# Seven conditional expert blocks, one after the other or one inside the other

## The chip, the cores and the metric

The kernel runs on one core of a Trainium2 chip. Its time is the device time of one execution, in microseconds (us); three executions of the kernel before took 800.02, 800.99 and 801.18 us, so the median is 800.99. A core has five engines that run their own instruction lists and wait for each other through semaphores: TensorE (PE, matmuls), VectorE (DVE), ScalarE (ACT), GpSimd (POOL, which also issues the gathers and scatters) and SyncE (SP, which issues the plain DMAs).

## What is computed

Three stages follow each other: a linear attention over four sequences of 576 positions, a gated dense layer, and a layer of eight experts of which each token uses one. The experts matter here. A token goes to the expert with the largest logit; each expert takes at most `capacity` tokens, 576 with these inputs:

```python
logits = x @ w_gate
expert_idx = np.argmax(logits, axis=1)
probs = softmax(logits);  gate_w = probs[np.arange(N), expert_idx]
# the first `capacity` tokens of each expert, in order, are kept
h = np.maximum(np.einsum('ecd,edf->ecf', disp, w1), 0.0)      # 512 -> 1024
y = np.einsum('ecf,efd->ecd', h, w2)                          # 1024 -> 512
out[i] = gate_w[i] * y[expert_idx[i], pos[i]]                 # 0 for tokens that are not kept
```

There are 2304 tokens. With these inputs four of the eight experts get 576 tokens each and the other four get none; no token is dropped. The kernel finds this out while it runs.

## The kernel before

Attention and the dense layer are written out as one long list of instructions without branches. While their last matmuls run, the tokens are routed: a table in DRAM gets for each expert the row numbers of its tokens, and a small tile `plan` gets the list of active experts, their counts and the number of active ones, `nact`.

The expert with the most tokens is worked on first, without a condition. The other experts are seven blocks in a Python loop, j = 1 to 7, each in a `tc.If(nact > j)` of its own (line 996). The number of the expert is read from `plan` by SP when its weights are loaded. With these inputs `nact` is 4: blocks 1, 2 and 3 are entered, 4 to 7 are not.

A block (`body`, L961) works on 256 + 320 rows of one expert in two calls of `part` (L188), the second in a condition on the count (L984). Each part runs over eight slices f of the 1024 hidden columns: a group of matmuls into `ph`, ScalarE's relu (L235) and VectorE's remainder (L238) into `h`, and the second group of matmuls from `h` into `yo`. Each float32 matmul is done as three matmuls of a high and a low half (`mm3`, L115 to L117). In between, `ew_dma` and `ew_split` load the next expert's weights and split them (`es`, `eu`, L123 to L135), `gather` fetches rows (`gr`, L167), and `turn` transposes them. A part ends with `emit` (L211): ScalarE scales `yo` into `y` (L214), and POOL scatters the rows of `y` into the output (L144). The last 64 rows are held as two halves; SP copies one half to the other's partitions (`z`, L217), VectorE adds them (L219).

The order of all instructions is the order in which the program is written (`manual_schedule`). Tiles come out of pools: 13 large `unit` buffers, 4 for `h`, 2 for weights on arrival, 2 for the tables, 5 + 3 PSUM banks, 7 for rows.

How a condition is built matters. Each engine has its own branch (COMPARE_AND_BRANCH). A block that is entered raises semaphores as its instructions end, and what follows the block waits for fixed counts. So an engine that skips a block runs a short list in its place, which raises the same semaphores by the same amounts: EVENT_SEMAPHORE instructions, and on POOL one INC_SWDGE_SEM for the semaphores of its own DMAs. It stands under the line of the condition, L996, and ends in an unconditional branch to what follows the block.

Of the kernel before, what the change touches and what calls it, by code (L numbers as in the profile page):

```python
# [8 lines left out]
F32 = mybir.dt.float32  # L9
F32R = mybir.dt.float32r  # L10
BF16 = mybir.dt.bfloat16
I32 = mybir.dt.int32
# [6 lines left out]
P = 128  # L19
B, H, S, D = 4, 8, 576, 64  # L20
NT = B * S
DM = H * D
DFF = 1536
NE = 8
FE = 1024
NC = DM // P
NFC = DFF // P
BLK = 384
# [4 lines left out]
RA = 256  # L33
RB = 320
# [33 lines left out]
go4.0 hl5.1* ac4.2 ac3.2* ac4.0*  # L68
"""
F64_MIN = struct.unpack("<f", struct.pack("<I", 897 << 20))[0]  # L70


def program(tc, ins, outs):
    nc = tc.nc
    ctx = ExitStack()
    with ctx:
# [4 lines left out]
        def unit(shape, dt, name):  # L81
            return units.tile(shape, dt, name=name, tag="unit")
# [20 lines left out]
        hp = ctx.enter_context(tc.tile_pool(name="hp", bufs=4))  # L103
        stg = ctx.enter_context(tc.tile_pool(name="stg", bufs=2))
        tbp = ctx.enter_context(tc.tile_pool(name="tbp", bufs=2))
        psa = ctx.enter_context(tc.tile_pool(name="psa", bufs=5, space=PSUM))
        pso = ctx.enter_context(tc.tile_pool(name="pso", bufs=3, space=PSUM))
# [58 lines left out]
        def gather(st, i, idx, g, n, rows=NT):  # L166
            nc.gpsimd.indirect_dma_start(  # L167
                out=g[:n],
                out_offset=None,
                in_=x2d[0:rows],  # L170
                in_offset=bass.IndirectOffsetOnAxis(ap=idx, axis=0),
                bounds_check=rows - 1,
                oob_is_err=False,
            )
            st[i] = g

        def turn(st, i, x, k, n=P):
            g = st.pop(i)
            pt = ps(f"tg{i}").rearrange("p (c t) -> p c t", c=NC)
            for c in range(NC):  # L180
                nc.tensor.transpose(pt[:, c, :n], g[:n, c * P : (c + 1) * P], ident[:n, :n])
            o = k * P
            nc.scalar.copy(x[:, :, 0, o : o + n], pt[:, :, :n])
            nc.vector.tensor_tensor(
                x[:, :, 1, o : o + n], pt[:, :, :n], x[:, :, 0, o : o + n].bitcast(F32), op=ALU.subtract
            )
# [74 lines left out]
        with ExitStack() as s2:  # L261
# [178 lines left out]
            def cb(f, i):  # L440
                tf, mag = ld["c", f, i]
                nc.vector.scalar_tensor_tensor(tf, mag, F64_MIN, tf, op0=ALU.is_ge, op1=ALU.mult)

# [254 lines left out]
            for token in FIRST.split():  # L698
                name = token.rstrip("*")
# [82 lines left out]
            for b in range(5):  # L782
                k = (4, 5, 7, 9, 11)[b]
# [12 lines left out]
            for i, (b, fs, mode) in enumerate(steps):  # L796
# [7 lines left out]
                k = i % NBLK  # L804
# [28 lines left out]
            xb = unit([P, NC, 2, 3 * P], F32R, "xb0")  # L833
# [60 lines left out]
        xgp = s3.enter_context(tc.tile_pool(name="xgp", bufs=2, reuse_waits="tile"))  # L894
        grp = s3.enter_context(tc.tile_pool(name="grp", bufs=7, reuse_waits="tile"))

        def g_tile(i):
            return grp.tile([P, DM], F32, name=f"gr{i}", tag="gr")

        def next_tables(e):  # L900
            st = {}
            fetch(st, "ta", e, 0, 2)
            fetch(st, "tb", e, RA, 2, rest=True)
            for i in range(2):
                gather(st, i, st["ta"][:, i, 0:1], g_tile(i), P)
            return st

        def turn_a(st):
            st["xa"] = xgp.tile([P, NC, 2, RA], F32R, name="xa", tag="xa")
            for i in range(2):  # L910
                turn(st, i, st["xa"], i)
# [4 lines left out]
        def work(ew, e, fs, lag):  # L916
            at = {}
            for i, f in enumerate(fs):
                at.setdefault(0 if i < 2 else lag[i - 2], []).append(lambda f=f: ew_dma(ew, e, f))
                at.setdefault(lag[i], []).insert(0, lambda f=f: ew_split(ew, f, both))  # L920
            return at

        def hooks(at, extra=None):
            def hook(f):
                if f == 0:
                    for w in at.get(0, ()):
                        w()
                if extra is not None:
                    extra(f)

            def after(f):
                if f > 0:
                    for w in at.get(f, ()):
                        w()

            return hook, after

        ew, st = {}, {}
# [19 lines left out]

        nact = st.pop("nact")

        def body(j, st, ew):  # L961
            more = j + 1 < NE
            cj = nc.values_load(plan[0:1, NE + j : NE + j + 1], min_val=0, max_val=NT)
            xb = unit([P, NC, 2, RB], F32R, "xb")
            nst, new = {}, {}

            def extra(f):
                if f == 0:
                    for i in range(3):
                        n = P if i < 2 else HALF  # L970
                        gather(st, 2 + i, st["tb"][:n, i, 0:1], g_tile(2 + i), n)
                if f == 1 and more:
                    nst.update(next_tables(nexp[j]))
                if 4 <= f <= 6:
                    turn(st, f - 2, xb, f - 4, P if f < 6 else HALF)
                if f == 7 and more:
                    turn_a(nst)

            half = work(new, nexp[j], range(4), (2, 4, 5, 6)) if more else {}
            part(st["xa"], RA, (P, P), ew, st["ta"], grp, "gr", *hooks(half, extra))  # L980
            if more:
                for k in (3, 4, 5):
                    new["u", k] = unit([P, 3, 2, 512], F32R, f"eu{k}")
            with tc.If(cj > RA) as big:  # L984
                half = work(new, nexp[j], range(4, 8), (1, 3, 5, 6)) if more else {}
                part(xb, RB, (P, P, HALF), ew, st["tb"], grp, "gr", *hooks(half))
            if more:
                with big.Else():
                    half = work(new, nexp[j], range(4, 8), (1, 2, 3, 4))
                    for f in range(5):  # L990
                        for w in half.get(f, ()):
                            w()
            return nst, new

        for j in range(1, NE):
            with tc.If(nact > j):  # L996
                st, ew = body(j, st, ew)


def layout(inputs):  # L1000
# [37 lines left out]
```

## Time and profile before

| | |
|---|---|
| median of three executions | 800.99 us |
| the profiled execution, its own time | 800.0 us |
| its span, first to last instruction | 798.2 us |
| TensorE busy | 759.5 us, 95% of the span |
| VectorE, ScalarE, GpSimd busy | 402.2, 278.8, 273.2 us |
| mean granted TensorE clock over the span | 0.987 |

The span is what the trace shows of one execution; 1.8 us of the execution's time lie around it. Branches and semaphore instructions are not counted as busy, so an engine may be idle in the table and still be at work in its instruction list. The view of one source line shows those instructions too, with a q behind the engine's name (POOLq, and PEldq for TensorE's list).

### The profile page before, as it was taken

What the parts mean: (1) busy time and instruction counts of PE and PEld (TensorE: products, weight loads), DVE (VectorE), ACT (ScalarE), POOL (GpSimd) and SP (SyncE); (2) the same over time, 40 slices, a digit from 0 to 9 for tenths busy, and PEclk for the clock granted to TensorE, in tenths of its full rate; (3) what the DMA queues carried; (4) which work ended last, traced back from release to release, by engine and by line L of the source; (5) the groups of instructions that cost most, each with busy time, mean ns of one, the idle gap of its engine ahead of it and who ended that gap; (6) DMA issues with size and microseconds to landing.
All of it is one profiled execution on the core that took longest, in us unless ns stands there. A gap on an engine that the chain in (4) does not pass through costs nothing. (4 is left out here: it accounts for less than half of the span.)

```text
span 798.2 us, 11945 instructions
## 1 busy us (share of the span) xinstructions
PE 759.5 (95%) x4400; PEld 698.0 (87%) x4400; DVE 402.2 (50%) x826; ACT 278.8 (35%) x537; POOL 273.2 (34%) x276
## 2 busy tenths in 40 slices
PE   6989999999999999999999999999999999999980
PEld 5988998999999999999989999999888888888870
DVE  7999966345454454544863323347724422433330
ACT  6756833322222222222332112223325533524430
POOL 5473713123232232322331313222535524425220
PEclk9999999999999999999999999999999999999995
DMA  9952020111010110101211011143255524515311
GB/s 305 364 172 83 28 79 28 31 53 53 27 54 27 53 50 31 53 28 53 80 67 40 2 41 41 53 134 117 62 150 176 191 80 127 159 53 182 129 41 37
DMA packets 34798, 70.53 MB, mean 88 GB/s; under 512 B 6528, under 2 KB 8704, under 8 KB 34720
## 3 DMA queue, kind: packets, MB, share of 16 engines
q1 hardware_dynamic: 31008, 59.40, 22.7%
q0 software_dynamic: 3712, 10.13, 4.0%
q8 instruction: 43, 0.70, 0.4%
q14 instruction: 35, 0.29, 0.1%
HBM read 59.45 MB, written 9.55 MB: 86 GB/s over the span
## 5 line engine op out<-in xcount | busy, mean ns | idle before, releaser
L491 POOL TENSOR_TENSOR h<-sg,h 128x384 fp32r<-128x384 f32 x70 | 77.6, 1110 | 242.5 <-ACT h L487 236.3
L483 DVE TENSOR_TENSOR sg<-sg,pv 128x384 f32<-128x384 f32 x72 | 39.7, 553 | 125.3 <-PE pv L117 100.6
L115 PE MATMUL pg<-xT,w 128*128 128x384 f32 x288 | 99.0, 344 | 0.0
L115 PE MATMUL pv<-xT,w 128*128 128x384 f32 x288 | 98.1, 341 | 0.1
L117 PE MATMUL pv<-xT,w 128*128 128x384 f32 x288 | 96.6, 336 | 1.5 <-POOL w L451 1.5
L116 PE MATMUL pg<-xT,w 128*128 128x384 f32 x288 | 96.7, 336 | 0.0
L117 PE MATMUL pg<-xT,w 128*128 128x384 f32 x288 | 96.5, 335 | 0.0
L116 PE MATMUL pv<-xT,w 128*128 128x384 f32 x288 | 96.4, 335 | 0.0
L117 PE MATMUL po<-w,h 128*128 128x512 f32 x216 | 86.0, 398 | 0.0
L115 PE MATMUL po<-w,h 128*128 128x512 f32 x216 | 85.2, 394 | 0.0
L116 PE MATMUL po<-w,h 128*128 128x512 f32 x216 | 85.1, 394 | 0.0
L479 ACT ACTIVATE sg<-pg 128x384 f32<-128x384 f32 x72 | 35.3, 490 | 129.4 <-PE pg L117 129.3
L451 POOL TENSOR_TENSOR w<-cv,w 128x512 fp32r<-128x512 f32 x34 | 45.1, 1325 | 98.7 <-ACT w L447 97.6
L487 ACT CAST h<-sg 128x384 fp32r<-128x384 f32 x68 | 34.9, 514 | 111.5 <-DVE sg L483 107.5
L238 DVE SCALAR_TENSOR_TENSOR h<-ph,h 128x64 fp32r<-128x64 f32 (+2 forms) x96 | 31.1, 354 | 84.0 <-ACT h L235 83.6
L135 POOL TENSOR_TENSOR eu<-es,eu 128x512 fp32r<-128x512 f32 x34 | 44.0, 1302 | 85.8 <-ACT eu L134 77.6
L521 DVE TENSOR_TENSOR acc<-acc,po 128x512 f32<-128x512 f32 x78 | 53.1, 687 | 36.5 <-PE po L117 35.3
L235 ACT ACTIVATE h<-ph 128x256 fp32r<-128x256 f32 (+3 forms) x64 | 26.3, 411 | 98.9 <-PE ph L117 61.0
L135 DVE TENSOR_TENSOR eu<-es,eu 128x512 fp32r<-128x512 f32 x46 | 43.1, 948 | 32.7 <-ACT eu L134 32.3
L117 PEld LDWEIGHTS pv<-xT,w 128*128 128x128 f32 x288 | 54.1, 188 | 2.2 <-POOL w L451 2.2
L116 PEld LDWEIGHTS pg<-xT,w 128*128 128x128 f32 x288 | 54.2, 188 | 1.3
L115 PEld LDWEIGHTS pg<-xT,w 128*128 128x128 f32 x288 | 54.1, 188 | 1.4
(201 smaller groups left out, 1667.9 us busy)
## 6 DMA issues: line engine op xcount, KB each, us to landing
es<-in_w SPq DMA_DIRECT2D x80, 256.0 KB, 3.4
s<-in_w SPq DMA_DIRECT2D x30, 512.0 KB, 3.4
q<-in_q SPq DMA_DIRECT2D x18, 256.0 KB, 7.0
x2d<-acc SPq DMA_DIRECT2D x6, 768.0 KB, 3.6
kt<-in_kT SPq DMA_DIRECT2D x3, 1152.0 KB, 8.1
vt<-in_v SPq DMA_DIRECT2D x3, 1024.0 KB, 15.0
raw<-in_w SPq DMA_DIRECT2D x6, 512.0 KB, 11.3
kt<-in_kT SPq DMA_DIRECT2D x4, 288.0 KB, 4.9
```

The costliest lines, as they stand in the source:

```text
L115: nc.tensor.matmul(out, l_hi, r_hi, start=start, stop=False)
L116: nc.tensor.matmul(out, l_hi, r_lo, start=False, stop=False)
L117: nc.tensor.matmul(out, l_lo, r_hi, start=False, stop=stop)
L135: engines[(i + f) % 2].tensor_tensor(u[:, 1], s[:, i], u[:, 0].bitcast(F32), op=ALU.subtract)
L235: nc.scalar.activation(h[:, 0, :used], ph[:, :used], AF.Relu)
L238: nc.vector.scalar_tensor_tensor(dst, ph[:, cols], 0.0, h[:, 0, cols].bitcast(F32), op0=ALU.max, op1=ALU.subtract)
L451: two[eng].tensor_tensor(w[:, i, 1, :], ld.pop(("c", f, i))[0], w[:, i, 0, :].bitcast(F32), op=ALU.subtract)
L479: nc.scalar.activation(pr, gt.pop(("g", b, f)), AF.Sigmoid)
L483: nc.vector.tensor_tensor(pr, pr, gt.pop(("v", b, f)), op=ALU.mult)
L487: alt[eng](h[:, 0], gt["r", b, f])
L491: two[eng].tensor_tensor(h[:, 1], gt.pop(("r", b, f)), h[:, 0].bitcast(F32), op=ALU.subtract)
L521: nc.vector.tensor_tensor(row(b, tt), row(b, tt), otile[b, tt], op=ALU.add)
```

## The change

The seven conditions are nested: block j + 1 stands inside block j, at its end. `chain` calls itself. Where an engine skips block 4, it branches past 5, 6 and 7 too, since they stand inside it: the list that takes the place of block 4 ends in a branch to the end of the kernel.

All tiles that the blocks use are now taken once, ahead of block 1. `Ring` hands out a fixed list of tiles in turn and has the method `tile` of a pool, so that the functions that call it stay as they are; `Tables` does this for the two tables. The number of buffers of each kind is the same as before: 6 + 6 `unit` tiles for two sets of weights and one for `xb`, 4, 2, 5, 3, 7 and 2 + 2 for the others.

```diff
+class Ring:
+    def __init__(self, tiles):
+        self.tiles, self.n = list(tiles), 0
+
+    def tile(self, shape, dt, name, tag):
+        self.n += 1
+        return self.tiles[(self.n - 1) % len(self.tiles)]
...
+        def ring(pool, n, shape, dt, tag, *first):
+            more = [pool.tile(shape, dt, name=f"{tag}r{i}", tag=tag) for i in range(n)]
+            return Ring([*more, *first])
+        sets = [
+            {k: u for k, u in ew.items() if k[0] == "u"},
+            {("u", k): unit([P, 3, 2, 512], F32R, f"ev{k}") for k in range(6)},
+        ]
+        xb1 = unit([P, NC, 2, RB], F32R, "xb1")
+        hp = ring(hp, 4, [P, 2, BLK], F32R, "h")
+        psa = ring(psa, 5, [P, 512], F32, "a")
...
         def body(j, st, ew):
...
-            xb = unit([P, NC, 2, RB], F32R, "xb")
-            nst, new = {}, {}
+            xb = xb1
+            nst, new = {}, dict(sets[j % 2])
...
-            if more:
-                for k in (3, 4, 5):
-                    new["u", k] = unit([P, 3, 2, 512], F32R, f"eu{k}")
...
-        for j in range(1, NE):
+        def chain(j, st, ew):
             with tc.If(nact > j):
-                st, ew = body(j, st, ew)
+                nst, new = body(j, st, ew)
+                if j + 1 < NE:
+                    chain(j + 1, nst, new)
+
+        chain(1, st, ew)
```

Lines move by 19 ahead of `body` and by 34 at the conditions: L984 becomes L1018, L996 becomes L1030, L1034 becomes L1072.

On POOL, at the end of block 6, the kernel before has this row. The four TENSOR_TENSOR are what the condition on the count does if it isn't met; the first ISA is its INC_SWDGE_SEM, and the second, at L996, that of the skipped block 6.

```order
L984 UNCONDITIONAL_BRANCH
L135 TENSOR_TENSOR eu_8928<-es_9181,eu_8928 128x512
L135 TENSOR_TENSOR eu_8928<-es_9184,eu_8928 128x512
L135 TENSOR_TENSOR eu_8929<-es_9191,eu_8929 128x512
L135 TENSOR_TENSOR eu_8929<-es_9198,eu_8929 128x512
L984 ISA
L984 UNCONDITIONAL_BRANCH
L996 ISA
L996 UNCONDITIONAL_BRANCH
L996 COMPARE_AND_BRANCH
L963 TENSOR_LOAD plan
L167 DMA gr_9225<-x2d,tb 128x512
```

The same place on POOL in the changed kernel:

```order
L1018 UNCONDITIONAL_BRANCH
L154 TENSOR_TENSOR eu_5629<-stgr_5752,eu_5629 128x512
L154 TENSOR_TENSOR eu_5629<-stgr_5753,eu_5629 128x512
L154 TENSOR_TENSOR eu_5704<-stgr_5752,eu_5704 128x512
L154 TENSOR_TENSOR eu_5704<-stgr_5753,eu_5704 128x512
L1018 ISA
L1018 UNCONDITIONAL_BRANCH
L1030 COMPARE_AND_BRANCH
L1000 TENSOR_LOAD plan
L186 DMA grr_5765<-x2d,tb 128x512
```

The work keeps its order; the list for the skipped block (L996 ISA and its branch) no longer stands between two blocks.

The end of POOL's list before, from the last block's scatters on; L1034 is the end of the kernel:

```order
L144 DMA out<-y_9651,tb 2304x512
L144 DMA out<-y_9659,tb 2304x512
L144 DMA out<-y_9641,tb 2304x512
L984 UNCONDITIONAL_BRANCH
L984 ISA
L984 UNCONDITIONAL_BRANCH
L996 ISA
L996 UNCONDITIONAL_BRANCH
L1034 ISA
```

And in the changed kernel, where seven pairs of ISA and branch stand behind each other, of which two are shown; the first takes the place of block 7, the last that of block 1 with all that it holds:

```order
L163 DMA out<-grr_5765,tb 2304x512
L163 DMA out<-grr_5766,tb 2304x512
L163 DMA out<-grr_5763,tb 2304x512
L1018 UNCONDITIONAL_BRANCH
L1018 ISA
L1018 UNCONDITIONAL_BRANCH
L1030 ISA
L1030 UNCONDITIONAL_BRANCH
L1030 ISA
L1030 UNCONDITIONAL_BRANCH
```

Every one of the seven branches goes to the end of the kernel, so an engine runs one of the seven lists. The lists for the skipped blocks have moved from between the blocks to the end, and the one for block 4 now raises the semaphores of blocks 4 to 7 together (by 64 to 80 each on POOL, where the one for block 4 before raised them by 16 to 32).

## Rows read from the trace of the kernel before

**Rows 1.** The page's first part: busy us (share of span) xinstructions
```profile
PE 759.5 (95%) x4400; PEld 698.0 (87%) x4400; DVE 402.2 (50%) x826; ACT 278.8 (35%) x537; POOL 273.2 (34%) x276
```

**Rows 2.** Stretches, each engine's busy us: blocks 1, 2, 3, the end
```profile
core 0: us, PE busy (x) PEld busy (x) DVE busy (x) ACT busy (x) POOL busy (x), PEclk, DMA share, GB/s
613.00:667.50 54.50, 54.50 (x329) 48.52 (x328) 20.09 (x38) 22.75 (x46) 21.82 (x19) 1.00 0.38 126
667.50:722.00 54.50, 54.25 (x326) 47.95 (x325) 19.61 (x38) 21.11 (x43) 20.25 (x18) 1.00 0.39 124
722.00:776.20 54.20, 54.01 (x322) 47.40 (x321) 19.56 (x38) 20.81 (x43) 20.70 (x18) 1.00 0.38 124
776.20:798.20 22.00, 0.00 (x0) 0.00 (x0) 0.68 (x1) 0.64 (x1) 3.37 (x3) 0.55 0.18 43
```

**Rows 3.** Timeline, PE: start us, us, engine, line, operation; the last matmul
```profile
775.72 0.39 PE L117 MATMUL yo<-eu,h 128*128 128x512 f32 x1
```

**Rows 4.** Timeline, POOL after 776 us: block 3's last scatters
```profile
776.41 1.00 POOL L144 DMA_INDIRECT out<-y,tb  x1 [5.27 <-ACT y L214]
...
779.48 0.92 POOL L144 DMA_INDIRECT out<-y,tb  x1 [0.30 <-issue]
```

**Rows 5.** L996 on POOL by stretch: duration ns min/median/max, first and last start
```profile
L996 POOLq COMPARE_BRANCH  x1: 45/45/45, 778.8 to 778.8; - x1
...
L996 POOLq EVENT_SEMAPHORE  x4: 17/43/43, 783.8 to 784.3; - x4
L996 POOLq INC_SWDGE_SEM  x1: 1371/1371/1371, 784.4 to 784.4; - x1
L996 POOLq COMPARE_BRANCH  x1: 45/45/45, 785.8 to 785.8; - x1
...
L996 POOLq INC_SWDGE_SEM  x1: 1353/1353/1353, 786.7 to 786.7; - x1
...
L996 POOLq INC_SWDGE_SEM  x1: 1353/1353/1353, 788.8 to 788.8; - x1
...
L996 POOLq INC_SWDGE_SEM  x1: 1353/1353/1353, 791.0 to 791.0; - x1
```

**Rows 6.** L1034, the end of the kernel, on POOL
```profile
L1034 POOLq EVENT_SEMAPHORE  x4: 17/17/17, 797.4 to 798.1; - x4
L1034 POOLq DRAIN  x3: 46/107/4960, 792.4 to 797.9; - x3
```

**Rows 7.** L996 and L1034 in TensorE's list, after 770 us
```profile
L996 PEldq COMPARE_BRANCH  x4: 3825/4421/5667, 773.8 to 788.8; - x4
...
L1034 PEldq DRAIN  x2: 8/8/8, 793.6 to 797.7; - x2
```

**Rows 8.** SP's waits after 776 us: us in total, times, longest
```profile
SPq L996 <- SPq L996: 8.4, 3, 4.0
SPq L1034 <- DMA out<-y,tb: 5.9, 1, 5.9
```

**Rows 9.** L942 on POOL, the skipped block for dropped tokens, and what follows it
```profile
L942 POOLq COMPARE_BRANCH  x1: 45/45/45, 599.2 to 599.2; - x1
L942 POOLq INC_SWDGE_SEM  x1: 728/728/728, 600.1 to 600.1; - x1
...
600.95 1.30 POOL L135 TENSOR_TENSOR eu<-es,eu 128x512 fp32r<-128x512 f32 x1 [1.33 <-DMA out<-y,ta]
```

**Rows 10.** L1026, the start of the kernel, on POOL
```profile
L1026 POOLq DRAIN  x1: 187/187/187, 0.3 to 0.3; - x1
```

**Rows 11.** Waits, 612 to 777 us: PE's, PEld's, VectorE's; SP's to the end
```profile
PE yo L117 <- DVE h L238: 0.3, 1, 0.3
...
PEld tg L181 <- issue: 1.1, 3, 0.4
PEld yo L117 <- DVE h L238: 0.7, 1, 0.7
...
DVE y L219 <- DMA z<-y: 8.7, 2, 5.0
...
SPq L217 <- ACT y L214: 38.0, 3, 12.9
```

**Rows 12.** Timeline, PE: the first matmuls of block 3, and its first `yo`
```profile
721.60 1.59 PE L229 MATMUL ph<-xa,eu 128*128 128x256 f32 x12
...
724.46 0.39 PE L115 MATMUL yo<-eu,h 128*128 128x512 f32 x1
```

More of the change, by code (lines that the diff above doesn't have):

```diff
@@ L70, with __init__, tile @@
 F64_MIN = struct.unpack("<f", struct.pack("<I", 897 << 20))[0]
+class Ring:
[4 more added lines that the diff above has]
+        return self.tiles[(self.n - 1) % len(self.tiles)]
+class Tables:
+    def __init__(self, ta, tb):
+        self.of = {"ta": ta, "tb": tb}
+    def tile(self, shape, dt, name, tag):
+        return self.of[tag].tile(shape, dt, name, tag)
 def program(tc, ins, outs):
@@ L959, in program @@
         nact = st.pop("nact")
+        def ring(pool, n, shape, dt, tag, *first):
[7 more added lines that the diff above has]
+        hp = ring(hp, 4, [P, 2, BLK], F32R, "h")
+        stg = ring(stg, 2, [P, 2, 512], F32, "stg")
+        psa = ring(psa, 5, [P, 512], F32, "a")
+        pso = ring(pso, 3, [P, 512], F32, "o")
+        grp = ring(grp, 7, [P, DM], F32, "gr")
+        xgp = ring(xgp, 1, [P, NC, 2, RA], F32R, "xa", st["xa"])
+        tbp = Tables(ring(tbp, 1, [P, 2, 4], I32, "ta", st["ta"]), ring(tbp, 1, [P, 3, 4], I32, "tb", st["tb"]))
         def body(j, st, ew):
```

## The prediction

> **What bounds the kernel now.** I began with the busy times of the engines: TensorE is at work for 95% of the span [rows 1], so at first sight only fewer matmuls could help, and the change keeps all of them. The table by stretch corrects this. In each of the three entered blocks TensorE is busy for 54.0 to 54.5 of some 54.3 us at a granted clock of 1.00, while the other engines have half their time free [rows 2]; there is next to nothing to gain inside a block. In the last 22.0 us of the span TensorE does nothing at all [rows 2]. Its last matmul starts at 775.72 and takes 0.39 us [rows 3], and the span ends at 798.2. So the kernel has two parts with different limits: up to 776.1 TensorE sets the pace, and behind it a tail of 22.1 us is set by something else.
>
> To see what, I followed POOL, the last to work. Its third scatter, the last one of the output, is issued from 779.48 to 780.40 [rows 4]. At 778.8 its instruction list had reached the condition of block 4, which isn't met. The list in its place first waits until the scatters have landed, which is over at 783.8 to 784.3, and then runs INC_SWDGE_SEM from 784.4 for 1.37 us [rows 5]. Three more conditions follow, and for each the same list: INC_SWDGE_SEM starts at 786.7, 788.8 and 791.0 and takes 1.35 us each time [rows 5]. At 792.4 POOL is through and begins a DRAIN of 4.96 us; at 797.4 it takes part in the barrier that ends the kernel, and 0.8 us later the span is over [rows 6]. TensorE's list skips the same four blocks in four branches of 3.8 to 5.7 us each and is through at 793.6 [rows 7], before POOL. SP's list loses 8.4 us at the same conditions [rows 8], and then waits for POOL. POOL's list is therefore the chain that ends last: scatter, landing, four skips, DRAIN, barrier.
>
> **The change part by part.**
> Three skips go. An engine that skips block 4 now branches to the end of the kernel. On POOL the part from the end of the first INC_SWDGE_SEM (784.4 + 1.37 = 785.8, where the next compare starts) to the DRAIN at 792.4 falls away [rows 5, 6]: 792.4 - 785.8 = 6.6 us, or three times 2.2. All of it lies on the path that sets the end, since nothing else of POOL is at work there.
>
> What is late next: TensorE and SP. TensorE reaches block 4's compare at 773.8, and it takes between 3.8 and 5.7 us [rows 7], so TensorE is through by 779.5, or by 785.2 if the branch out of the short list costs as much once more. SP must see the semaphores that POOL raises at 785.8; in the profile before it waits there for POOL, 5.9 us, put down to the scatter [rows 8]. POOL's DRAIN would end at 785.8 + 5.0 = 790.8, five microseconds after these, so neither takes over.
>
> The DRAIN is the term with the least ground. It takes 4.96 us behind four skips, though the scatters have landed eight microseconds earlier; the DRAIN at the start of the kernel takes 0.19 [rows 6, 10]. If each INC_SWDGE_SEM left a fourth of it behind, one would leave 1.24 and 3.7 us more would go. If it did not depend on them, it stays at 4.96. I take 4.96: the one other INC_SWDGE_SEM inside the kernel, at L942, ends at 600.8, and POOL's next operation starts at 600.95 [rows 9]; one of them leaves at most 0.15 us of work behind, and four would leave 0.6. Both ends stay in the range.
>
> The one list that is left raises the semaphores by more: 64 to 80 each, where one list before raised them by 16 to 32. If INC_SWDGE_SEM took as long as its amounts, the one would cost what the four did, 4 x 1.36 = 5.4 instead of 1.37, and 4.1 of the 6.6 us would come back. At L942 the amounts are 32 to 48, about twice those of the skips, and it is the shorter one, 0.73 against 1.35 [rows 5, 9]. I take no growth and keep 4.1 as the other end.
>
> The jump is longer. Block 4's list used to stand behind one block; now it stands behind four. On TensorE skips of one block cost 3.8 to 5.7 us of branch [rows 7]; on POOL block 4's skip began at 778.8 and its first semaphore instructions ran before the scatters landed [rows 5]. A branch of 5.7 us on POOL would end at 784.5, against 783.8, when the wait for the scatters ends anyway. The landing covers a jump of up to 5.0 us, and 0.7 us shows at worst. [...]
>
> Inside the blocks. The order of the work on every engine stays; the number of buffers of each kind too. The waits change in number: the first gather of a block waits for fewer semaphores, some of ScalarE's and VectorE's instructions for one more. These are 17 to 50 ns on lists that have half their time free. What of it could show is TensorE's waiting, and in 165 us that is 0.3 us on VectorE at the start of block 2, 0.7 us of weight loads for the same reason and 1.1 us at the transposes [rows 11]. If the change removed all of these it would gain 2.1; as the wait at the start of block 2 comes from VectorE standing behind the copy `z` (8.7 us for two of them [rows 11]), and this order stays, I take 0, and -0.5 to +0.5 as the bounds. Between blocks an entered block no longer jumps over the list for the skipped one; TensorE's list runs ahead of its matmuls there (no gap at 667 or 722 [rows 2, 11]), so this is worth nothing.
>
> **The sum.** The span of the profiled execution becomes 798.2 - 6.6 = 791.6, and its time 800.0 - 6.6 = 793.4. The profiled execution is at the low end of the three; the median is 0.99 higher. From the median: 801.0 - 6.6 = **794.4 us**.
>
> **The rivals.**
> *A, the forecast:* three skips of POOL go, the DRAIN stays. 794.4; with the terms above (-0.5 to +0.5 inside the blocks, up to +0.7 for the jump) 793.9 to 795.6, and with half of the 1.2 us between the three executions 793.3 to 796.2.
> *B, the DRAIN shrinks with the skips:* for it, 4.96 behind four skips against 0.19 without; against it, the operation behind L942's INC_SWDGE_SEM is not late. 794.4 - 3.7 = 790.7.
> *C, INC_SWDGE_SEM grows with its amounts:* for it, the equal times at nearly equal amounts; against it, L942. 794.4 + 4.1 = 798.5.
> *D, no change:* the DRAIN ends at a fixed time behind the last scatter, as work that POOL does whatever its list holds; then the barrier comes at 797.4 as before, and the time is 801.0. For it, that the DRAIN waits for something which is nowhere in the trace; against it, that two later DRAINs are short [rows 6], and that TensorE's, beside it, takes 8 ns. [...]
> *E, slower:* the wait at the start of a block grows. VectorE stands behind the copy `z` at a block's end, with up to 5.0 us of waiting [rows 11], and TensorE wants VectorE's `h` for the first `yo`, 2.9 us into the next block [rows 12]. Were the copy issued later, because SP still waits for a buffer of the weights that it loads ahead of it, TensorE would stop at the starts of blocks 2 and 3. SP now stands ready at the copy for about 12.7 us before `y` exists, three times [rows 11]; beyond that, each microsecond counts twice. To eat the 6.6 us the weights would have to come 12.7 + 3.3 = 16 us later in both blocks; at 18 the time would be 801.0 + 2 x 5.3 - 6.6 = 805.0. Against it: SP's DMAs stand in the same order, with the same number of buffers.
>
> **How the numbers follow.** A 0.66, B 0.14, C 0.08, D 0.08, E 0.04. The likeliest gives 794.4. A and B hold 0.80, and C is the bound of an unknown cost, so the range goes from B, less 0.5 and 0.6 as for A, 789.6, to C, 798.5. What a measurement of this kernel can tell from no change is about 0.2%, 1.6 us: faster means below 799.4. A, B and C are, 0.88; D is within; E is slower.
>
> **What would show it.** In the profile of the changed kernel POOL should have one INC_SWDGE_SEM at the line of the conditions, of 1.3 to 1.4 us (C: over 5), right behind the landing of the last scatter, and the DRAIN some 1.4 us later, of 5.0 us (B: about 1.2; D: ending some 13 us behind the landing). TensorE should have one long compare behind the last matmul instead of four. The last matmul should still end at 776 within 0.5 us; if it comes over 3 us later, E is right. The tail from there to the span's end should be 15.5 us. The prediction is wrong if POOL's chain isn't the last any more, above all if TensorE's second branch, out of the short list, takes longer than 10 us.

## The result

The changed kernel takes 793.07 us (median; 791.39 to 794.54), the kernel before in the same measurement 801.09 us (800.02 to 803.14). The ratio is 0.9896, with a 95% interval from 0.9867 to 0.9926. The forecast was 794.4 us with a range from 789.6 to 798.5. Two more measurements of the same pair, further down, gave 0.9906 and 0.9908: a gain of 0.9 to 1.0%, 7 to 8 us where 6.6 were forecast.

The profiled execution took 791.39 us, its span is 789.5. The stretches (us, busy us of each engine, granted clock, share of the DMA engines, GB/s), as in [rows 2]:

```profile
613.00:667.50 54.50, 54.50 (x331) 48.52 (x330) 20.61 (x38) 22.80 (x46) 22.41 (x20) 1.00 0.39 126
667.50:722.00 54.50, 54.17 (x326) 47.85 (x325) 19.47 (x38) 20.74 (x43) 20.20 (x19) 1.00 0.38 124
722.00:775.80 53.80, 53.70 (x322) 47.38 (x320) 19.57 (x38) 20.63 (x43) 20.75 (x18) 1.00 0.39 125
775.80:789.50 13.70, 0.00 (x0) 0.00 (x0) 0.68 (x1) 0.63 (x1) 2.90 (x3) 0.66 0.20 59
```

The three blocks are as full as before: TensorE is busy for all but 0.4 us of the three stretches, at a granted clock of 1.00. What has changed is the last row, 13.7 us instead of 22.0. The timelines of TensorE and POOL show where the tail begins [rows 3, 4]:

```profile
775.31 0.39 PE L136 MATMUL or<-eu,hr 128*128 128x512 f32 x1
```

```profile
777.31 0.99 POOL L163 DMA_INDIRECT out<-grr,tb  x1 [0.30 <-issue]
778.70 0.92 POOL L163 DMA_INDIRECT out<-grr,tb  x1 [0.41 <-DVE grr L238]
```

And POOL's list from there on, at the line of the conditions (L1030) and at the end of the kernel (L1072); durations in ns, then first and last start [rows 5, 6]:

```profile
L1030 POOLq EVENT_SEMAPHORE  x6: 17/30/43, 781.6 to 782.1; - x6
L1030 POOLq COMPARE_BRANCH  x2: 43/46/50, 778.6 to 783.6; - x2
L1030 POOLq INC_SWDGE_SEM  x1: 1370/1370/1370, 782.1 to 782.1; - x1
```

```profile
L1072 POOLq DRAIN  x3: 46/107/4962, 783.7 to 789.2; - x3
```

There is one INC_SWDGE_SEM of 1.37 us instead of four, the DRAIN of 4.96 us right behind it, and the barrier. TensorE's list has one long compare of 4.3 us instead of four and is through more than 10 us before POOL is at the barrier [rows 7]; SP's wait at the end is again put down to POOL's scatters [rows 8]:

```profile
L1030 PEldq COMPARE_BRANCH  x2: 184/2236/4288, 773.4 to 778.0; - x2
...
L1072 PEldq DRAIN  x2: 8/8/8, 778.3 to 789.0; - x2
```

```profile
SPq L1072 <- DMA out<-grr,tb: 4.7, 1, 4.7
```

The chain of POOL in pieces, in us, from the starts and semaphore events of the two traces to two digits. A scatter has landed when its last semaphore event shows:

| piece | before | after | difference |
|---|---|---|---|
| start of the last matmul | 775.72 | 775.31 | -0.41 |
| from there to the start of the last scatter | 3.76 | 3.39 | -0.37 |
| to its last landing | 4.60 | 2.80 | -1.80 |
| to the first INC_SWDGE_SEM | 0.29 | 0.65 | +0.36 |
| to the DRAIN | 8.05 | 1.56 | -6.49 |
| to the end of the span | 5.81 | 5.81 | 0.00 |
| **span** | 798.23 | 789.52 | **-8.71** |

The row of -6.49 is the forecast. The 1.80 us of landing were not in the sum. The view of the scatters themselves shows them as well (from issue to landing, in us; the last scatter's are 4.6 and 2.8), before and after:

```profile
DMA to landing us min/median/max: 3.2/4.6/6.1
```

```profile
DMA to landing us min/median/max: 2.8/3.2/3.7
```

### The profile page after: what moved, and what is told of

Read it like the earlier page. It is cut to its first block, busy times and chain, and to the rows that moved or that the text cites. A ratio compares the mean times of both kernels' runs of the same rounds, so it can differ in the third digit from the quotient of the medians.

```text
span 789.5 us, 11894 instructions
## 1 busy us (share of the span) xinstructions
PE 760.4 (96%) x4400; PEld 698.2 (88%) x4400; DVE 402.8 (51%) x826; ACT 278.7 (35%) x537; POOL 273.6 (35%) x276
## 4 chain that ended last, share of the span: by engine, by line
PE 77%; DVE 8%; issue 6%; DMA 2%; ACT 2%; POOL 2%; SPq 1%; DVEq 0%; POOLq 0%; ACTq 0%
PE po L136 6%; PE po L135 6%; PE po L134 6%; PE pv L134 6%; PE pg L134 6%; PE pv L136 6%; PE pv L135 6%; PE pg L135 5%; PE pg L136 5%; PE ar L134 2%; PE ar L136 2%; PE ar L135 2%; PE or L136 2%; PE or L134 2%; PE or L135 2%
## 5 line engine op out<-in xcount | busy, mean ns | idle before, releaser
L257 DVE SCALAR_TENSOR_TENSOR hr<-ar,hr 128x64 fp32r<-128x64 f32 (+1 forms) x72 | 23.4, 354 | 78.1 <-ACT hr L254 78.0
L136 PEld LDWEIGHTS pv<-xT,w 128*128 128x128 f32 x288 | 54.1, 188 | 2.2 <-POOL w L470 2.2
L134 PEld LDWEIGHTS pg<-xT,w 128*128 128x128 f32 x288 | 54.1, 188 | 1.4
L135 PEld LDWEIGHTS pg<-xT,w 128*128 128x128 f32 x288 | 54.2, 188 | 1.3
L134 PEld LDWEIGHTS pv<-xT,w 128*128 128x128 f32 x288 | 54.1, 188 | 0.5 <-issue 0.4
L135 PEld LDWEIGHTS pv<-xT,w 128*128 128x128 f32 x288 | 54.1, 188 | 0.0
L136 PEld LDWEIGHTS pg<-xT,w 128*128 128x128 f32 x288 | 54.1, 188 | 0.0
## 6 DMA issues: line engine op xcount, KB each, us to landing
vt<-in_v SPq DMA_DIRECT2D x3, 1024.0 KB, 14.3
```

Of the source, the lines that this page charges most:

```text
L134: nc.tensor.matmul(out, l_hi, r_hi, start=start, stop=False)
L135: nc.tensor.matmul(out, l_hi, r_lo, start=False, stop=False)
L136: nc.tensor.matmul(out, l_lo, r_hi, start=False, stop=stop)
L257: nc.vector.scalar_tensor_tensor(dst, ph[:, cols], 0.0, h[:, 0, cols].bitcast(F32), op0=ALU.max, op1=ALU.subtract)
```

## The experiments

Three theories stood at first. Theory 1, of the prediction: each skipped block costs about 2.2 us of POOL's list at the end. Theory 2: the tiles that are taken once make the blocks shorter. Theory 3: the skips that follow fetch instructions while the last scatters land, and hold them up.

Ratios are to the kernel before beside which a kernel was measured, with the 95% interval; they are not the quotients of the medians in the table. The median of the kernel before was 801.90 us beside the first four variants (rings_flat to short), 800.49 beside the next four (nocond to after_again) and 800.36 beside the last four. "Tail" is the time from the start of the last matmul to the end of the span in the profiled execution; "landing" is from the start of the last scatter to its last semaphore event.

| kernel | us | ratio | last matmul | tail | 2nd scatter, ns | landing |
|---|---|---|---|---|---|---|
| before | 801.09 | | 775.7 | 22.5 | 1453 | 4.60 |
| after | 793.07 | 0.9896 | 775.3 | 14.2 | 987 | 2.80 |
| rings_flat | 801.81 | 0.9994 (0.9974 to 1.0013) | 780.5 | 22.3 | 1442 | 4.37 |
| tail_nest | 794.18 | 0.9911 (0.9881 to 0.9941) | 779.1 | 14.7 | 1402 | 3.19 |
| two_skips | 805.53 | 1.0021 (0.9993 to 1.005) | 788.7 | 18.6 | 977 | 4.85 |
| short | 800.13 | 0.997 (0.9943 to 0.9997) | 785.4 | 14.3 | 987 | 3.12 |
| nocond | 788.13 | 0.9835 (0.9802 to 0.9867) | 776.8 | 10.2 | 1119 | 2.63 |
| tiny_dma | 798.60 | 0.9973 (0.9957 to 0.9989) | 778.2 | 19.3 | 977 | 2.98 |
| tiny_plain | 793.56 | 0.9903 (0.9871 to 0.9935) | 778.3 | 14.8 | 987 | 2.75 |
| after_again | 793.67 | 0.9906 (0.9874 to 0.9937) | 776.6 | 14.9 | 987 | 3.18 |
| after_third | 792.43 | 0.9908 (0.989 to 0.9926) | 775.2 | 15.3 | 987 | 3.01 |
| two_skips_again | 796.60 | 0.9964 (0.9949 to 0.9979) | 776.1 | 18.5 | 978 | 4.95 |
| short_again | 792.42 | 0.9907 (0.989 to 0.9923) | 776.3 | 14.0 | 977 | 2.91 |
| rings_flat_again | 799.22 | 0.9991 (0.9975 to 1.0007) | 776.7 | 22.0 | 1377 | 4.20 |

### The tiles alone

Here the tiles are taken once, and the conditions stand one after the other:

```diff
-        def chain(j, st, ew):
-            with tc.If(nact > j):
-                nst, new = body(j, st, ew)
-                if j + 1 < NE:
-                    chain(j + 1, nst, new)
-
-        chain(1, st, ew)
+        for j in range(1, NE):
+            with tc.If(nact > j):
+                st, ew = body(j, st, ew)
```

> The rings of the change with the seven conditions one after the other again. Theory 1 (the time is in GpSimd's list at the end: 2.2 us for each skipped block, one after the other): four skips as before, four INC_SWDGE_SEM of 1.35 us and 801 us, the last matmul at 775.7. Theory 2 (the rings' waits make the blocks shorter): the last matmul 0.4 us or more earlier than before, as in the changed kernel, and up to 1.3 us of the gain remain, 799.7. Theory 3 (the skips set off fetches of instructions beside the last scatters, which land later): the last scatter lands at about 784 as before, some 3.6 us behind its issue, and 801.

Measured: ratio 0.9994, no difference, and the tail of before, 22.3 us with four INC_SWDGE_SEM. The intervals, here and in the repetition below, would still hold the 1.3 us of Theory 2. But the last matmul isn't earlier than before (780.5, in the repetition 776.7, against 775.7), and in the three profiles of the changed kernel it starts at 775.2 to 776.6, on both sides of before. So Theory 2 has nothing to show; the gain comes with the nesting.

### The nesting where it matters

Blocks 1 to 3 one after the other, only 4 to 7 nested:

```diff
+        for j in range(1, 4):
+            st, ew = chain(j, st, ew, j)
+        chain(4, st, ew, NE - 1)
```

(`chain` gets the last block of its nest as an argument, and returns `nst, new`.)

> Blocks 1 to 3 one after the other, blocks 4 to 7 nested. Theory 1: one skip at the end, so as the changed kernel, 793.1, one INC_SWDGE_SEM. If nesting the entered blocks mattered, it would be nearer to 794 or 795. Theory 3: the last scatter lands within 2 us of its issue, as in the changed kernel.

Measured: ratio 0.9911, tail 14.7. What counts is the number of lists that are run at the end, not the nesting of the entered blocks. The second scatter takes 1.40 us on POOL here as in before, and not 0.99 as in the changed kernel, and still the tail is as short.

### One more list

Blocks 1 to 4 nested, then 5 to 7 nested: two lists run.

```diff
+        st, ew = chain(1, st, ew, 4)
+        chain(5, st, ew, NE - 1)
```

> Blocks 1 to 4 nested in each other, then blocks 5 to 7 nested in each other: two skips at the end. Theory 1: 2.2 us more than the changed kernel, 795.3, two INC_SWDGE_SEM. If the three skips were not alike (a later one is cheaper or free): 793.1 to 794. Theory 3: the second jump is a further fetch; the last scatter may land up to 2 us later, and 795.3 to 797.

And the same without blocks 5 to 7, which these inputs don't need (`short` leaves them out, so it computes no more than five active experts):

```diff
+        chain(1, st, ew, 4)
```

> Blocks 1 to 4 nested, blocks 5 to 7 left out (they are never entered with these inputs): one skip, over one block instead of four. Theory 1 with the jump hidden under the landing of the scatters: 793.1. If the longer jump is what GpSimd waits for (3.0 us from its compare to the next instruction in the changed kernel), its list starts as soon as the scatters have landed, 0.1 to 0.3 us earlier there, and 792.8; were the jump free and the landing not behind it, 790.5.

Both came out far too slow: 805.5 and 800.1 us. But their tails are those of Theory 1, 18.6 and 14.3 us. The loss lies before the tail: the last matmul is late by 13 and 10 us. Set beside the trace of before, matmul by matmul, both kernels lose nearly all of this time in two places, just behind the starts of blocks 2 and 3, and run nearly level everywhere else: between 667 and 735 us two waits of ScalarE without a releaser make up 11.3 us in `two_skips` and 10.7 in `short`. (The profiled executions took 809.9 and 801.6 us.) ScalarE's timeline in `two_skips` shows the first:

```profile
680.21 0.38 ACT L254 ACTIVATE hr<-ar 128x256 fp32r<-128x256 f32 x1 [8.49 <-remote]
```

The third relu of the block waits 8.5 us for a semaphore of TensorE, whose last matmul for it had started at 674.2; the event of that semaphore shows at 680.1. "remote" means that the trace has no releaser for it. The four kernels above were measured together, and their traces have something else in common: about a fifth of the landing events of the DMAs is missing (3142 to 3213, against 3900 to 3918 in all other profiles). All four also have such waits of ScalarE without a releaser behind 612 us, 18.4 us in `two_skips`, 18.6 in `short`, 14.3 in `rings_flat` and 3.8 in `tail_nest`; no other profile has one. And in `rings_flat` and `tail_nest` too the last matmul is late, by 5 and 3 us. So there were two readings: something held up the engines in this one set (Theory 4), or it belongs to the programs (Theory 5). All of them but `tail_nest` were measured again, beside the changed kernel.

> Blocks 1 to 4 nested, then 5 to 7 nested: two lists are run for skipped blocks. Theory 1 (2.2 us for each list on POOL) with Theory 4: last matmul at 775 to 778.5 and a tail of 17 to 19 us, so some 796 us and a ratio of 0.993 to 0.996. Theory 5: the last matmul is late again, at 785 or later, and the time is 802 to 806, a ratio of about 1.002.

> Blocks 1 to 4 nested, and blocks 5 to 7 left out, which these inputs do not need: one list. Theory 1 with Theory 4: as the changed kernel, 793 to 794 us, ratio 0.990, last matmul at 775 to 778.5. Theory 5: the last matmul at 782 or later, 798 to 801 us, ratio 0.997.

> The tiles taken once, the seven conditions one after the other as before. Theory 1 with Theory 4: last matmul at 775 to 778.5, a tail of 22 us, 800 to 802 us, ratio 0.998 to 1.001. Theory 5 (here: the last matmul 5 us late belongs to this program, so that the rings cost time which the nesting gives back): last matmul at 780 or later, ratio 1.000 or above.

> The changed kernel once more, beside the three that follow. The runs two_skips and short had their last matmul at 788.7 and 785.4 us, where the changed kernel had it at 775.3 and 776.6; in both, ScalarE's third relu of blocks 2 and 3 stood up to 8.8 us for TensorE's semaphore. Theory 4 (the time of the runs, not the program: something held up the engines at the starts of the blocks while these were measured): the ratio stays at 0.990, or all four kernels of this set are late together. Theory 5 (a property of those two programs): ratio 0.990 here, last matmul at 775 to 778.5, tail from the last matmul's start to the end 14 to 15 us.

All four speak for Theory 4 and against a fixed property of the programs. The last matmul comes at 775.2 to 776.7 in each, the landing events are complete again (3905 to 3916), and the waits without a releaser are gone: in `two_skips_again` the longest wait of this relu for TensorE between 667 and 735 us is

```profile
ACT hr L254 <- PE ar L136: 19.0, 11, 3.2
```

(us in total, times, longest us). `short_again` is as fast as the changed kernel, 0.9907 against 0.9908. `two_skips_again` takes 796.60 us, 4.2 more than `short_again`, for one list. Its INC_SWDGE_SEM and those of `rings_flat_again`:

```profile
L1030 POOLq INC_SWDGE_SEM  x2: 1353/1362/1371, 784.8 to 787.3; - x2
```

```profile
L1030 POOLq INC_SWDGE_SEM  x4: 1353/1353/1371, 784.9 to 791.5; - x4
...
L1068 POOLq DRAIN  x3: 46/107/4960, 792.9 to 798.4; - x3
```

In `two_skips_again` the second list starts 2.5 us behind the first, and in `rings_flat_again` four stand in (791.5 - 784.9) / 3 = 2.2 us each. The other 2 us of `two_skips_again` are its landing, 4.95 against 2.91 us.

What held up the engines in the first set was not found, nor why it cost `two_skips` and `short` the most. The repetitions ran on another chip than the first set, so it is also open whether it went with the time or with that chip; the second four were measured on the first set's chip and show none of it. Records were missing and engines stood in the same four profiles; that the one has to do with the other no run shows.

### What a skip costs without its block

Behind the changed kernel's chain stand three more conditions that aren't met, each holding one scatter (`tiny_dma`), or a memset of VectorE in its place (`tiny_plain`):

```diff
+        for i in range(3):
+            with tc.If(nact > 4):
+                scatter(outs["out"], dropi[:, i : i + 1], grp.tiles[i], NT, "out")
```

```diff
+        for i in range(3):
+            with tc.If(nact > 4):
+                nc.vector.memset(grp.tiles[i], 0.0)
```

> The changed kernel with three more conditions behind it, each around one scatter of GpSimd that is never run: three more skips of nearly nothing, close to each other in the list. Theory 1: each skip is paid by GpSimd's INC_SWDGE_SEM and the waits around it, 1.4 to 2.2 us, whatever was skipped: 793.1 + 4.2 to 6.6 = 797.3 to 799.7. If a skip is paid by the length of the jump (the size of the skipped block): under 1 us for the three, 793.1 to 794.

> The changed kernel with three more conditions behind it, each around one memset of VectorE, with no DMA in them. Theory 1: no INC_SWDGE_SEM is needed, so a skip costs GpSimd only its compare and one or two semaphore instructions, 0.2 to 0.4 us each: 793.1 + 0.6 to 1.2 = 793.7 to 794.3. If every skip costs GpSimd the same 2.2 us: 799.7.

> The changed kernel once more, beside the two with more conditions. Theory 1: 793.1, one INC_SWDGE_SEM of 1.37 us and a DRAIN of 4.96. Theory 3: its last scatter lands within 2 us of its issue again; if it lands 3.6 us behind, the earlier landing was chance, and the gain is 6.6 and not 8.

POOL in `tiny_dma`, then in `tiny_plain`, at the three conditions:

```profile
L1038 POOLq INC_SWDGE_SEM  x3: 1335/1339/1345, 786.9 to 790.2; - x3
```

```profile
L1038 POOLq COMPARE_BRANCH  x3: 45/45/50, 786.8 to 787.1; - x3
```

`tiny_plain` is as fast as the kernel without the three conditions (793.56 against 793.67): a skip costs POOL 0.16 us if no DMA of POOL stands inside. With one scatter inside it costs (798.60 - 793.56) / 3 = 1.7 us, of which 1.34 are INC_SWDGE_SEM. It is nearly as long for one scatter as for four blocks (1.37 us), so here its time doesn't follow the amounts. With a whole block in the condition the skip costs 2.2 us. What sets the time of INC_SWDGE_SEM is open: the one ahead of the blocks takes 0.73 us [rows 9], and one at the start of the kernel, at L1026 in before, 0.03.

### No conditions at the end

Blocks 1 to 3 stand without conditions, and 4 to 7 are left out; this kernel is right only where exactly four experts are active:

```diff
+        for j in range(1, 4):
+            st, ew = body(j, st, ew)
```

> Blocks 1 to 3 without a condition, blocks 4 to 7 left out: no skip at the end at all (the condition on the count inside a block stays, and the skipped block for dropped tokens near 600 us). Theory 1: the INC_SWDGE_SEM of 1.37 us and its waits go, and the jump; 793.1 - 1.4 = 791.7, or 791 if the landing was waiting on the jump; the DRAIN stays at 4.96 us. If the DRAIN is put-off work of INC_SWDGE_SEM: it falls to 0.2 us and the time to 786.7. If the landing delays it (a DRAIN that waits for the scatters): it begins earlier and ends where it ended.

Ratio 0.9835, 5.5 us below the changed kernel measured beside it. POOL's last scatter and its DRAIN:

```profile
780.17 0.92 POOL L163 DMA_INDIRECT out<-grr,tb  x1 [0.30 <-issue]
```

```profile
L1067 POOLq DRAIN  x3: 46/112/6853, 779.2 to 786.6; - x3
```

The DRAIN starts at 779.2, while the scatters are still being issued, takes 6.85 us and ends at 786.1, which is 5.0 us behind the end of the last scatter's issue (780.17 + 0.92 = 781.09). So the five microseconds are not work that INC_SWDGE_SEM leaves behind: they come here too, where none is near. Everywhere else the DRAIN starts with POOL's work done and takes 4.96 us from its start, also in `tiny_plain`, where it starts 0.66 us behind the end of INC_SWDGE_SEM. What POOL does in them isn't shown. With no list to run, nothing of POOL waits for the landing either, which is over at 782.8, and the two lie beside each other.

## Why the prediction was right

**What bounds the kernel.** Confirmed. Over the three profiles of the changed kernel the last matmul starts at 775.2 to 776.6, against 775.7 before, and the tail is 14.2 to 15.3 us (14.8 in the mean) against 22.0 to 22.5 in the three profiles with four lists of whole blocks. The whole gain lies behind the last matmul. The 15.5 us expected there were counted from the matmul's end, 0.4 us later; from there it measured 13.8 to 14.9.

**Three skips go: -6.6.** Confirmed at -6.49 in the trace, and in dose: one list 14.0 to 15.3 us of tail, two 18.5 and 18.6, four 22.0 to 22.5; none 10.2. The steps hold more than the lists: some 2 us between one and two are the landing.

**The DRAIN stays at 4.96.** Confirmed: 4.96 behind one, two and four lists. Rival B would have had 1.24 behind one. The reason given was that L942's INC_SWDGE_SEM leaves next to nothing behind; `nocond`, with a DRAIN that ends 5.0 us behind POOL's last work and no such instruction near it, bears this out.

**INC_SWDGE_SEM doesn't grow.** Confirmed: 1.37 us for the amounts of four blocks, 1.34 for one scatter. Rival C falls.

**Rival D, no change,** falls with the first three steps. A skip without DMAs of POOL does cost POOL little, 0.16 us in `tiny_plain`, with a compare of 0.05. The price of POOL's other skips, 1.7 to 2.2 us, is the list and not the compare.

**Rival E, slower,** falls: SP stands ready at the copy of the halves for 13.5 us at the longest, where it was 12.9 [rows 11]:

```profile
SPq L236 <- ACT grr L233: 40.3, 3, 13.5
```

**The jump: 0 to +0.7.** What shows of it lies inside the bounds, but the two numbers behind them were both too large: a jump of 5.7 us under a landing that gives cover for 5.0. From POOL's compare to the first instruction of the list it takes 3.0 us in the changed kernel (778.63 to 781.60), 3.4 and 3.5 in the two repetitions, against 0.17 in before; in `short_again`, whose list stands behind one block, 0.5. The landing now covers 2.9 us from the compare on, so the list starts when the jump is over, 0.1 us after the landing and not before it, and INC_SWDGE_SEM comes 0.65 us behind the landing instead of 0.29: +0.36, and +0.5 to +0.6 in the repetitions. The 3.0 us stand behind four blocks and the 0.5 behind one; what POOL does in them isn't shown.

**The step that was mis-sized: the landing.** The sum let the scatters land as before, 4.60 us behind the start of the last one, and saw in the landing only the cover for the jump. It measured 2.80, a gain of 1.80, and is why the gain is 7 to 8 us and not 6.6. Over the three profiles of either kind (four lists, and the changed kernel) the mean landing goes from 4.39 to 2.99, -1.40; the jump gives back 0.47, the lists are -6.49, and the tail is shorter by 7.45. The way from the last matmul to the last scatter, 0.37 us shorter in the first profile, is 3.73 and 3.69 in these means: the faster second scatter (1453 to 987 ns) brings nothing that lasts. Forecast A's own bounds, 793.3 to 796.2, missed the median by 0.2 us; the range held it because its lower end was set for rival B, whose reason didn't come true. That much is luck. The table sorts the landing by one thing: where a skip of a whole block follows block 4's (before, rings_flat, two_skips, and the two repetitions) it takes 4.20 to 4.95 us, in all nine other profiles 2.63 to 3.19. The DMA view from the first scatter to INC_SWDGE_SEM (queue: packets, MB, share of the DMA engines) shows the instruction packets of one queue that run beside it. First `two_skips_again`, then the changed kernel:

```profile
q8 instruction: 2, 0.03, 3.4%
```

```profile
q8 instruction: 1, 0.02, 1.0%
```

This packet of 16 KB is there twice in each of the five profiles with a long landing, once in eight others and not at all in `nocond`, which has the shortest. In the five, TensorE's list stands in its second long compare, of 5.3 to 5.7 us, while the scatters land (in before from 778.0 to 783.7); in the others it is at the end of the kernel by then. In the last 25 us of all profiles one or two packets of this queue start within each of TensorE's long compares, 0.1 to 1.3 us behind its start (in before 0.4 to 1.1, in the changed kernel 0.2 and 1.0). The skips of `tiny_dma` and `tiny_plain`, over one scatter or memset, take TensorE 0.2 us each and leave the landing short, at 2.98 and 2.75 us. This fits Theory 3: TensorE, already at the next skip, seems to fetch its list while the scatters land. That these packets are what holds the scatters up is argued from this and not shown, since no run moved the fetches alone. That POOL issues the second scatter faster goes with something else: it takes 1.38 to 1.45 us in the four profiles in which a list for the skipped block stands right behind block 3 (before, rings_flat twice, tail_nest), and 0.98 to 1.12 in the others. Why was not tried.

## What to carry to other kernels

Look behind the last matmul: a kernel with TensorE at work for 95% of its span still had 22 us in which it did nothing, and the gain was there alone. A condition that isn't met cost little by itself here (0.16 us on POOL), but 1.7 us where it held one DMA of POOL and 2.2 us where it held a whole block, and 4.2 where scatters were still landing (`two_skips_again` beside `short_again`). Nest such conditions, so that one list is run for all, or keep DMAs of POOL out of conditions that come last; the second was seen only in `tiny_plain`. And before a slow variant is explained, see in its trace where the time went: two kernels lost 10 and 13 us in a stretch that the edit didn't touch, and had them back when measured again, on another chip.

## What the hardware showed beside that

POOL's DRAIN at the end of the kernel takes 4.96 us in every kernel with a list, and runs beside the landing of the scatters if no list stands between (6.85 us in `nocond`). So the one list that the changed kernel keeps, with the conditions of blocks 1 to 3, still costs some 5 us: `nocond` is 5.5 us shorter, 4.8 of them in the tail, where the 1.6 from INC_SWDGE_SEM to the DRAIN and the wait for landing and jump in front of it, 3.0 us behind the last scatter's issue, go. A kernel for any number of active experts without that list at its end was not tried.
